# Two attention layers on one core: the second layer's output projection as Strassen products at the end, and log-sum rows by transfers

## The chip, the cores and the metric

The kernel runs on one core of one Trainium2 chip. The core has a matrix engine (TensorE, PE in the profile, with its weight loads shown apart as PEld), a vector engine (VectorE, DVE), a scalar engine (ScalarE, ACT), GpSimd (POOL) and a queue engine (SyncE, SP). SP, ACT and POOL issue DMA transfers, which 16 DMA engines carry out. The metric is the device time of one execution in microseconds; less is better.

## The reference

Two independent attention layers, A and B, each with an input `x` of 2048 x 1024, a `wqkv` of 1024 x 3072 and a `wo` of 1024 x 1024, all float32, with 32 heads of 32 features.

```
qkv = (x @ wqkv).reshape(B, S, 3, H, Dh)            # q, k, v per head
A: each position sees 8 keys: itself and every second position before it
   logits = q . k * scale, softmax over the 8, weighted sum of v, then @ wo
B: each position sees itself and the 255 before it
   scores = q . k * scale, masked, softmax, weighted sum of v, then @ wo
result = concat([a, b], axis=-1)
```

Both projections `@ wo` are full 2048 x 1024 by 1024 x 1024 matrix products. For A, the host sorts positions into even and odd ones, so that "every second position" becomes a plain window of 8 neighbours.

## The kernel before

**Units and groups.** The work is cut into 8 units of 512 positions: units 0 to 3 are layer B (`dense`), units 4 to 7 layer A (window of 8). A unit has 8 groups (`NG`) of four heads; a group is numbered `hg` = 8u + s. For each unit the program makes q and k per group (`qk_items`, L518), v in three parts (`v_items`, L583), attention per group, and the output projection (`o_items`, L645).

**Precision by three terms.** Each float32 operand of a large product is held as a high part and a low part in TensorE's faster type. `parts` (L195 to L209) makes them: a cast by ScalarE (L201) or VectorE (L204), then subtractions on VectorE (L207, 512 columns at a time). Every product is then three matmuls (`TERMS`): high x high, high x low, low x high.

**The stream of operands.** `Stream` holds the list of all weights and inputs in the order of their use, each item 128 x 1024 floats (512 KB). `load_to` issues a load on POOL's queue (L159) into one of three buffers (`raws`, `NRAW` = 3); `split_to` splits it into `wpool` (three tiles) or `xpool` (nine half tiles); when the split is over, the buffer takes the next load.

**Attention of layer B.** Per group, a first pass (`first`, L857) makes 16 score blocks, VectorE adds the mask and takes row maxima (L862), ScalarE sums the exponentials (L867). `log_sum` turns maximum and sum into one number per row, as a high and a low part (L885 to L888). `rows` turns these to lie along the free axis by a matmul with the identity (L896), and `spread` writes them as rows 96 to 127 of the stacked q, one VectorE multiplication for each of four heads (L902). A second pass (`second`, L940) of 128 rows then gives transposed scores less their log-sum in one matmul, ScalarE's exponential (L947) gives probabilities, GpSimd or VectorE clears what is masked (L926, L929), and L987 multiplies by v. The stacked q and k (`qst`, `kst`, two of each) are filled by SP's transfers out of `nat` (L479), halo reads (L408) and writes (L469).

**Attention of layer A.** `window`: q and k are seated by SP's transfers (L438), 128 small matmuls score (L711), VectorE and ScalarE do the softmax (L719 to L749), ScalarE spreads it (L758, L761), and L774 multiplies by v.

**Output.** `finish` splits each group's outcome into high and low (L822 on ScalarE, L826 on VectorE) in one of ten tiles of `opool`. The projection of unit u-1 runs between the groups of unit u (`O_SLOTS`), 8 outputs of 24 matmuls each; the last unit's projection stands at the very end, where four of its outputs are started without their last step (`TAIL`). `copy_out` (L536, L539) takes a finished output out of PSUM, and ACT's queue stores it.

**What sets the order.** A planner in the program (`Clock`, and the loop from L1060) knows a duration for each kind of work and writes all engines' instructions in the order of its due times. It takes from four lists: the long products (`gemm`), first passes, second passes, and the row matmuls. On the chip each engine runs its instructions in that written order and waits by semaphores.

Of the kernel before, what the change touches and what calls it, by code (L numbers as in the profile page):

```python
# [7 lines left out]
F32 = mybir.dt.float32  # L8
# [19 lines left out]
ROWS_LATE, KEYS_LATE = 0, 1.2  # L28
# [6 lines left out]
TAIL, XAT = 4, 1  # L35
# [95 lines left out]
class Stream:  # L131
# [3 lines left out]
    def __init__(self, nc, ck, raws, wpool, xpool, items, more, light):  # L135
# [4 lines left out]
        self.loaded = self.split = 0  # L140
# [3 lines left out]
    def load_to(self, n):  # L144
        while not self.loaded:
# [7 lines left out]
            self.loaded = 2  # L153
        while self.loaded < min(n, len(self.items)):
            k = self.loaded - NRAW
# [7 lines left out]
    def split_to(self, n):  # L163
# [12 lines left out]
        while self.split < min(n, len(self.items)):  # L176
            i = self.split
            self.load_to(i + 1)
            raw, t0 = self.raw.pop(i)
            if self.items[i][0] != "w":  # L180
                self.tiles[i], self.ready[i] = [], []
                for h in range(2):
                    t = self.xpool.tile([P, 2, S], F32R, tag="x", name="x")
                    self.ready[i].append(self.parts(t, raw[:, h * S:(h + 1) * S], t0, i < SIDE))
                    self.tiles[i].append(t)
# [31 lines left out]
def kernel(ctx, tc, xs, wqk, wv, wo, outs, units):  # L217
# [3 lines left out]
    U = len(units)  # L221
    units, xs = [units[i] for i in ORDER], [xs[i] for i in ORDER]
# [5 lines left out]
    natp = ctx.enter_context(tc.tile_pool(name="natp", bufs=NN))  # L228
    pickp = ctx.enter_context(tc.tile_pool(name="pickp", bufs=1))
    opool = ctx.enter_context(tc.tile_pool(name="opool", bufs=NO))  # L230
# [13 lines left out]
    for u in range(U):  # L244
        for s in range(NG):
            if u and s in O_SLOTS:
                plan += [("o", u - 1, n) for n in O_SLOTS[s]]
# [6 lines left out]
    plan += [("o", U - 1, n) for n in range(NG)]  # L254
    items, where = [], {}

# [13 lines left out]
    for p in plan:  # L270
        ly = units[p[1]][0]
        if p[0] == "o":
            item(p, "w" if p[1] < U - 1 or p[2] < 3 else "xw", wo[ly, p[2]])
# [25 lines left out]

    qst = [stackp.tile([P, 4, S], F32R, tag=f"q{i}", name=f"qst{i}") for i in range(2)]  # L300
# [4 lines left out]
    def constants():  # L305
# [13 lines left out]
        pick = cst["pick"] = pickp.tile([32, 16], F32, name="pick")  # L319
        nc.gpsimd.memset(pick, 0.0)  # L320
        for row in (0, 16):
            nc.gpsimd.affine_select(pick, pick, pattern=[[-1, 16]], compare_op=ALU.not_equal, fill=1.0, base=-row,
                                    channel_multiplier=1)
# [14 lines left out]
        def ones():  # L338
            zero = cst["mask_d"][96:P, None, P:2 * P].to_broadcast([32, 24, P])
            for t in kst:  # L340
                nc.scalar.activation(t[96:P, :, :].rearrange("p j (a s) -> p (j a) s", s=P), zero, AF.Identity,
                                     bias=1.0, scale=1.0)
                ck.use("act", 2.7, ck.now)
# [12 lines left out]
    xt, xready, ot, rows = {}, {}, {}, {}  # L356
    done, waiting = {}, {}
    for k in ("stack", "v", "o", "ot", "out", "nat", "second", "clear", "scores"):
        done[k] = {}
# [36 lines left out]
    def qk_items(u, s):  # L396
# [100 lines left out]
        for t in range(2):  # L497
# [15 lines left out]
            def run(k, t=t, h=h):  # L513
# [6 lines left out]
                if k == ASK and st.items[min(where["qk", u, s, t] + 1, len(st.items) - 1)][0] != "x":  # L520
                    st.split_to(where["qk", u, s, t] + 2)
# [100 lines left out]
    def o_items(u, n):  # L622
        h = {}

        last = u == U - 1
        ring = rs if last and n == 3 else rg

        def ready(k):
            if (u * NG + k) not in done["ot"]:
                return None  # L630
            if k == 0:
# [3 lines left out]
                return latest(ring.when(), h["r"][0], done["ot"][u * NG])  # L635
            return max(done["ot"][u * NG + k], h["r"][k // 4])

        def run(k):
            if k == 0:
                h["ps"], h["b"] = ring.take()  # L640
# [6 lines left out]
            if k == ASK and (not last or n == 0 or n > 2):  # L647
                st.split_to(where["o", u, n] + (3 if last and n == 0 else 2))
            if k == 5 and last and n in (1, 2):
                st.split_to(where["o", u, n] + 3)  # L650

        def after(k):
            if k == NK - 1:
# [3 lines left out]
                o = pbuf[:, n % 4, :S] if last else stp.tile([P, S], F32, tag="ost", name="ost")  # L657
                e = copy_out(o, h["ps"], h["b"], ring)
# [9 lines left out]
        return [(lambda k=k: ready(k), lambda k=k: run(k), 3 * CG, lambda k=k: after(k)) for k in range(NK)]  # L668

# [461 lines left out]
```

## Time and profile before

| | |
|---|---|
| median of 3 runs | 1832.38 us (1831.74 to 1832.67) |
| profiled execution, first to last instruction | 1830.6 us |
| TensorE busy | 1807.8 us, 99% |
| VectorE busy | 1202.9 us, 66% |
| ScalarE busy | 889.4 us, 49% |
| GpSimd busy | 394.4 us, 22% |
| DMA | 257.43 MB, 141 GB/s on average |

The profiled execution's own time is given by the page as its span only, 1830.6 us from the first to the last instruction; the three timed runs are other executions, 1.8 us longer in the median. A row of the groups by line has the line, engine and operation, what is written from what with the shapes, the count, then the busy time and the mean of one, then the idle time of the engine before them and what ended it. A row of the waits has who waited for whom, us in total, times, and the longest. A row of the timeline has start, length, engine, line, operation and count, with the idle time before it in brackets. A row of a DMA issue has the tile, the queue, the count, the size of one and the median us from issue to landing. A matmul's duration is modelled and overlaps the next one.

### The profile page before, as it was taken

The numbers are of one execution on the slowest core, as the hardware profiler recorded it, in microseconds if no ns is written. First come the engines' busy times: TensorE is split into PE (matmuls) and PEld (weight loads), VectorE is DVE, ScalarE is ACT, GpSimd is POOL, SyncE is SP. The second block draws the span as 40 slices with busy tenths as digits, with TensorE's granted clock in tenths as the row PEclk, the third lists the DMA queues.
The fourth block names the chain that finished last, engine by engine and source line by source line (L and its number), as shares of the span: only waits on it lengthen the run. The fifth ranks groups of instructions, "written<-read, shape, count | busy, mean of one in ns | idle before, by whom it ended". The sixth has DMA issues, their size and how long they took to land.

```text
span 1830.6 us, 38331 instructions
## 1 busy us (share of the span) xinstructions
PE 1807.8 (99%) x14826; PEld 1477.5 (81%) x14826; DVE 1202.9 (66%) x2694; ACT 889.4 (49%) x2254; POOL 394.4 (22%) x926
## 2 busy tenths in 40 slices
PE   9999999999999999999999999999999999999998
PEld 7787777888778888788887788888888788888887
DVE  6677886768867669777777564655547445655463
ACT  5556466565655655656555343433425234423331
POOL 3322323233242324332233200110001000100000
PEclk9999999999999999999999999999999999999999
DMA  8455665545656456455554343444334443534432
GB/s 242 121 138 139 176 164 150 170 121 160 164 155 164 136 151 183 125 157 141 141 142 130 110 135 116 152 143 130 119 115 143 133 138 108 162 107 128 127 104 83
DMA packets 109141, 257.43 MB, mean 141 GB/s; under 512 B 14496, under 2 KB 29856, under 8 KB 108960
## 3 DMA queue, kind: packets, MB, share of 16 engines
q0 software_dynamic: 41760, 152.06, 28.1%
q1 hardware_dynamic: 56832, 83.00, 17.6%
q10 hardware_dynamic: 10368, 19.93, 3.0%
q8 instruction: 117, 1.92, 0.5%
q14 instruction: 64, 0.52, 0.1%
HBM read 164.63 MB, written 23.07 MB: 103 GB/s over the span
## 4 chain that ended last, share of the span: by engine, by line
PE 92%; DVE 4%; DMA 2%; ACT 2%; issue 1%; SPq 0%; ACTq 0%; POOL 0%; DVEq 0%; POOLq 0%
PE g L518 37%; PE g L645 19%; PE g L583 17%; PE s L940 5%; PE s L857 5%; PE o L987 5%; PE s L711 2%; PE o L774 2%; DMA raw<-xs 1%; DVE w L207 1%; DVE s L862 1%; ACT s L867 0%; DMA qst<-nat 0%; DMA pbuf<-nat 0%; DVE x L207 0%
## 5 line engine op out<-in xcount | busy, mean ns | idle before, releaser
L518 PE MATMUL g<-x,w 128*128 128x512 f32 x3072 | 770.2, 394 | 3.8 <-DVE nm L729 2.4
L518 PEld LDWEIGHTS g<-x,w 128*128 128x128 f32 x3072 | 566.3, 189 | 114.2 <-issue 8.3
L583 PE MATMUL g<-w,x 128*128 128x256 f32 (+1 forms) x2304 | 391.9, 320 | 0.9 <-issue 0.7
L207 DVE TENSOR_TENSOR w<-raw,w 128x512 fp32r<-128x512 f32 x516 | 338.6, 698 | 52.0 <-ACT w L201 44.8
L583 PEld LDWEIGHTS g<-w,x 128*128 128x128 f32 x2304 | 332.3, 190 | 29.2 <-DVE w L207 1.8
L645 PE MATMUL g<-ot,w 128*128 128x512 f32 x1416 | 343.6, 393 | 3.7 <-DVE ot L826 1.8
L867 ACT ACTIVATE s<-s,nm 128x384 f32<-128x384 f32 (+2 forms) x512 | 274.3, 536 | 102.1 <-DVE nm L862 101.8
L862 DVE CUSTOM_DVE_ANT_0 s<-s,mask_d 128x384 f32<-128x384 f32 (+2 forms) x512 | 261.5, 553 | 88.2 <-PE s L857 87.5
L645 PEld LDWEIGHTS g<-ot,w 128*128 128x128 f32 x1416 | 262.4, 188 | 59.3 <-DVE ot L826 3.2
L926 POOL TENSOR_SCALAR_AFFINE_SELECT pbuf<-pbuf 128x128 f32<-128x128 f32 (+1 forms) x606 | 219.8, 391 | 325.1 <-ACT pbuf L947 323.8
L947 ACT ACTIVATE pbuf<-s 128x384 f32<-128x384 f32 (+2 forms) x480 | 202.7, 505 | 72.2 <-PE s L940 70.2
L159 POOL DMA_DIRECT2D raw<-wqk x126 | 68.1, 540 | 457.5 <-DVE w L207 356.3
L204 DVE CAST w<-raw 128x1024 fp32r<-128x1024 f32 x205 | 141.7, 691 | 24.8 <-PE g L518 24.0
L940 PEld LDWEIGHTS s<-qst,kst 128*128 128x128 f32 x704 | 113.0, 188 | 41.2 <-ACT s L867 16.3
L857 PE MATMUL s<-kst,qst 96*128 96x384 f32 (+2 forms) x512 | 142.4, 342 | 0.9 <-ACT s L867 0.6
L940 PE MATMUL s<-qst,kst 128*128 128x256 f32 (+2 forms) x704 | 136.5, 302 | 3.5 <-ACT s L867 3.0
L719 DVE TENSOR_TENSOR band<-s,near 128x160 f32<-128x160 f32 x128 | 32.4, 315 | 158.0 <-PE s L711 158.0
L536 ACT COPY ost<-g 128x512 f32<-128x512 f32 x54 | 31.7, 587 | 207.1 <-PE g L645 200.4
L857 PEld LDWEIGHTS s<-kst,qst 96*128 96x128 f32 x512 | 93.4, 189 | 26.2 <-issue 4.7
L826 DVE TENSOR_TENSOR ot<-o,ot 128x512 fp32r<-128x512 f32 x64 | 44.0, 688 | 101.6 <-ACT ot L822 101.4
L867 ACT ACTIVATION_READ_ACCUMULATOR s<-s,nm 128x1 f32 x512 | 105.3, 206 | 0.0
L159 POOL DMA_DIRECT2D raw<-wo x64 | 34.2, 534 | 304.2 <-DVE w L207 260.2
(77 smaller groups left out, 1298.6 us busy)
## 6 DMA issues: line engine op xcount, KB each, us to landing
raw<-wqk POOLq DMA_DIRECT2D x126, 512.0 KB, 4.3
raw<-wv POOLq DMA_DIRECT2D x72, 512.0 KB, 5.1
raw<-wo POOLq DMA_DIRECT2D x64, 512.0 KB, 4.1
qst<-nat SPq DMA_DIRECT2D x96, 256.0 KB, 5.3
kst<-nat SPq DMA_DIRECT2D x96, 256.0 KB, 5.6
raw<-xs POOLq DMA_DIRECT2D x28, 512.0 KB, 4.6
outs<-ost ACTq DMA_DIRECT2D x56, 256.0 KB, 2.3
kst<-halo SPq DMA_DIRECT2D x72, 128.0 KB, 4.5
```

Source lines behind the costliest of these rows:

```text
L159: (self.nc.scalar if early else self.nc.gpsimd).dma_start(raw if len(ap.shape) == 2 else raw.rearrange("p (a b) -> p a b", a=2), ap)
L204: nc.vector.tensor_copy(t[:, 0, :], raw)
L207: nc.vector.tensor_tensor(t[:, 1, c:c + 512], raw[:, c:c + 512], t[:, 0, c:c + 512].bitcast(F32), op=ALU.subtract)
L518: nc.tensor.matmul(h["ps"], h["w"][:, a, k * P:(k + 1) * P], xt[u][k][:, b, :], start=(k == 0 and i == 0), stop=(k == NK - 1 and i == 2))
L583: nc.tensor.matmul(ps, xt[u][kw * g + k][:, a, p0:p0 + P], h["w"][g][:, c, k], start=(first and t == 0 and half == 0), stop=(last and t == 2),
L645: nc.tensor.matmul(h["ps"], w[:, a, c:c + P], ot[u, k][:, b, :], start=(k == 0 and i == 0), stop=(k == NK - 1 and i == 2))
L857: nc.tensor.matmul(ps[:, :n], q[0:96, j, b * P:(b + 1) * P], kk[0:96, j, c0:c1], start=True, stop=True)
L862: nc.vector.tensor_tensor_reduce(ps[:, :n], ps[:, :n], mask[:, cut:full], scale=-1.0, scalar=BIG, op0=ALU.add, op1=ALU.min, accum_out=nm)
L867: nc.scalar.activation(ps[:, :n], ps[:, :n], AF.Exp, bias=nm, scale=-1.0, accum_out=sm)
L926: nc.gpsimd.affine_select(w, w, pattern=[[0, m], [step, n]], compare_op=ALU.is_ge, fill=0.0, base=base, channel_multiplier=chan)
L940: nc.tensor.matmul(ps[:, i * n:(i + 1) * n], kk[:, j, 256 + kb * P:256 + (kb + 1) * P], q[:, j, q0:q0 + n], start=True, stop=True)
L947: nc.scalar.activation(w, ps[:, :pack * n].rearrange("p (j n) -> p j n", j=pack), AF.Exp)
```

## The change

Two things change.

**Layer A's projection.** Units 4 and 5, and units 6 and 7, form pairs. In a pair, the outputs of attention are a matrix of 2 x 2 blocks (unit by half of the 1024 features), and so is `wo` (half of the features by half of the outputs). Of the eight block products only seven are made, out of blocks and sums of blocks, by a Strassen scheme (`PRODUCTS`), and added up into four blocks (`product`). Each product is 4 x 4 x 3 = 48 matmuls. All 14 stand at the end of the program. Outputs of layer A's attention are therefore not split at once: `finish` copies them out and SP stores them to DRAM (`od`). Sums of them (`output_sums`) and of `wo` (`weight_sums`) are made in the background by tasks of two loads, four VectorE operations and two stores (`background`), into `sd` and `td`, after unit 3's projection and whenever two units' outputs are stored. The products' operands come through the stream: two items of outputs or sums and two of weights or sums for each product; `gates` hold back a load in the written order until what it reads is stored. Finished blocks leave by ACT's queue out of three tiles in turn, or out of the tile in which they were added up. Unit 3's projection is spread over units 4 and 5 (`O_LATE`).

**Log-sum rows.** `spread` no longer multiplies. It copies the 32 x 128 outcome of the row matmul to one small tile, by ScalarE or VectorE, and SP copies it by four transfers into 8 rows (96 to 103) of the stacked q, one for each head. The rows of the stacked k that meet them hold ones only for the head's own two rows, and the second pass reads 104 rows instead of 128. The planner adds 2.0 us to the landing of each row transfer (`ROWS_LATE`).

Ten tiles of a new pool (`slot`) take the place of `opool` and serve outputs, sums, totals and outgoing tiles.

```diff
-ROWS_LATE, KEYS_LATE = 0, 1.2
+ROWS_LATE, KEYS_LATE = 2.0, 1.2
-TAIL, XAT = 4, 1
+PRODUCTS = (("11", "11"), ("12", "21"), (0, 3), (2, 2), ("22", 1), (3, 0), (1, "22"))
+O_LATE = {4: {2: (0, 1), 3: (2, 3)}, 5: {2: (4, 5), 3: (6, 7)}}
+BG_REST, BG_SLACK = 2.0, 1.5
...
-    plan += [("o", U - 1, n) for n in range(NG)]
+    plan += [("p", u, i) for u in range(DU, U, 2) for i in range(7) if u > DU or i not in O_AT.values()]
...
+    def product(u, i):
...
+        def run(n, k):
+            if k == 0:
+                h["ps"], h["b"] = rg.take()
+            w, x = held["t", u, i, n // 2][0], held["s", u, i, k // 2][0][k % 2]
+            c = S * (n % 2) + P * k
+            for t, (a, b) in enumerate(TERMS):
+                nc.tensor.matmul(h["ps"], w[:, a, c:c + P], x[:, b, :], start=(k == 0 and t == 0),
+                                 stop=(k == 3 and t == 2))
+            if k == 1:
+                at = where["p", u, i, "t", 1]
+                more_w = [kind for kind, _ in st.items[at + 1:at + 1 + (n + 1 if n else 0)]]
+                while more_w.count("w") > 1 + n // 2:
+                    more_w.pop()
+                st.split_to(at + 1 + len(more_w))
...
+            if i in (1, 4):
+                where_o["ot"] += 1
+                o = slot(2 + where_o["ot"] % 2)[:, :S] if where_o["ot"] % 3 else stp.tile([P, S], F32, tag="ost", name="ost")
+            if i == 0:
+                nc.scalar.copy(a, ps)
+                e = ck.use("act", 0.485, ck.now + ck.SEM)
+            elif i == 1:
+                e = add(o, a)
+                store(0, 0, o, e)
+            elif i == 2:
+                e = add(a, a)
+            elif i == 3:
+                e = add(c, a)
+            elif i == 4:
+                e = add(o, c)
+                store(1, 0, o, e)
+            elif i == 5:
+                e = add(c, c)
+                store(1, 1, c, e)
+                e = add(a, a)
+            else:
+                e = add(a, a)
+                store(0, 1, a, e)
+            rg.give(bank, e)
...
+    def background():
...
+        loads, ops, dst, key, who = bg["tasks"].pop(0)
+        t = [slot(4 + 2 * lane + z).rearrange("p (a s) -> p a s", a=2) for z in range(2)]
+        for c, ap in loads:
+            nc.sync.dma_start(t[c // 2], ap)
+            e = ck.copy("load", ck.now)
+
+        def add():
+            for to, x, y, op in ops:
+                nc.vector.tensor_tensor(*[t[c // 2][:, c % 2, :] for c in (to, x, y)], op=op)
+                e = ck.use("dve", 0.64, ck.now, port=True)
+            ck.defer(e, put)
+
+        def put():
+            for z in range(2):
+                nc.sync.dma_start(dst[:, 2 * z:2 * z + 2, :], t[z])
...
     def finish(u, s, h):
-        o = opool.tile([P, 2, S], F32R, tag="ot", name="ot")
+        if u >= DU:
+            o = slot(2 + hg % 2)[:, :S]
+            nc.scalar.copy(o, h["o"])
...
+                nc.sync.dma_start(od[u][:, s, :], o)
...
+                    if s >= 4 and u % 2:
+                        output_sums(u - 1, s - 4)
...
+            return
+        o = slot(hg).rearrange("p (a s) -> p a s", a=2).bitcast(F32R)
...
             def spread():
-                for j in range(4):
-                    nc.vector.tensor_tensor(q[96:P, j, :].rearrange("p (b s) -> p b s", s=P),
-                                            ps[0:32, None, 0:P].to_broadcast([32, 4, P]),
-                                            cst["pick"][0:32, 4 * j:4 * j + 4, None].to_broadcast([32, 4, P]), op=ALU.mult)
+                row = rowp.tile([32, P], F32R, tag="row", name="row")
+                if ck.ends("act", 0.22, ck.now) <= ck.ends("dve", 0.2, ck.now):
+                    nc.scalar.copy(row, ps[0:32, 0:P])
...
+                else:
+                    nc.vector.tensor_copy(row, ps[0:32, 0:P])
...
+                def place():
+                    h["rows"] = []
+                    for j in range(4):
+                        nc.sync.dma_start(q[96:104, j, :].rearrange("r (b s) -> r b s", s=P).bitcast(F32),
+                                          row.bitcast(F32))
+                        h["rows"].append(ck.copy("part", e, ck.now) + ROWS_LATE)
...
-                nc.tensor.matmul(ps[:, i * n:(i + 1) * n], kk[:, j, 256 + kb * P:256 + (kb + 1) * P],
-                                 q[:, j, q0:q0 + n], start=True, stop=True)
+                nc.tensor.matmul(ps[:, i * n:(i + 1) * n], kk[0:104, j, 256 + kb * P:256 + (kb + 1) * P],
+                                 q[0:104, j, q0:q0 + n], start=True, stop=True)
```

More of the change, by code (lines that the diff above doesn't have):

```diff
@@ L178, in split_to @@
             self.load_to(i + 1)
+            if i not in self.raw:
+                return
             raw, t0 = self.raw.pop(i)
@@ L221 @@
     U = len(units)
+    DU = sum(u[2] for u in units)
     units, xs = [units[i] for i in ORDER], [xs[i] for i in ORDER]
@@ L354 @@
     halo = [[dram.tile([P, 2, 256], F32, name=f"halo{i}_{s}") for s in range(NG)] for i in range(2)]
[L356 to L359, printed above, removed]
+    xt, xready, ot, rows, waiting = {}, {}, {}, {}, {}
     class Ring:
```

208 lines of the change are left out of this document (168 added, 40 removed).

## The prediction

> **What bounds the kernel now.** I read the page first: the busy shares, the granted clock, the chain that ended last.
>
> ```profile
> span 1830.6 us, 38331 instructions
> PE 1807.8 (99%) x14826; PEld 1477.5 (81%) x14826; DVE 1202.9 (66%) x2694; ACT 889.4 (49%) x2254; POOL 394.4 (22%) x926
> PEclk9999999999999999999999999999999999999999
> PE 92%; DVE 4%; DMA 2%; ACT 2%; issue 1%; SPq 0%; ACTq 0%; POOL 0%; DVEq 0%; POOLq 0%
> ```
>
> TensorE is busy for 99% of the span at full clock and carries 92% of the chain; the other engines have room on average. So a matmul taken away shortens the time, if nothing new makes TensorE wait. The span is 1.8 us under the median of the three runs (1832.38); I sum on the span and add 1.8.
>
> Next the timeline of TensorE at the end, for what one matmul costs when they follow each other closely and what the end loses; then its waits by releaser.
>
> ```profile
> 1786.00 7.54 PE L645 MATMUL g<-ot,w 128*128 128x512 f32 x32 [1.12 <-DVE ot L826]
> 1804.96 21.92 PE L645 MATMUL g<-ot,x 128*128 128x512 f32 x96
> ```
> ```profile
> PE s L896 <- DVE hl L888: 3.6, 4, 2.0
> PE s L940 <- ACT s L867: 3.0, 4, 1.1
> PE g L518 <- DVE nm L729: 2.4, 1, 2.4
> ```
>
> 96 matmuls of 512 columns in 21.92 us are 0.228 us each, though the rows give each 394 ns: they overlap. The waits are few. Two lie at the end: 2.4 us (the one wait on L729, in the last unit's attention) and 1.12 us before the projection. The 3.6 and 3.0 us lie in layer B, around the log-sum rows and the second pass.
>
> **The change, part by part.**
>
> *Matmuls.* Layer A's projection was 4 units x 8 x 8 x 3 = 768 matmuls of 512 columns; seven products for each of two pairs are 14 x 4 x 4 x 3 = 672. The built order shows exactly 96 fewer, every other matmul is still there, so a change that does not do what it says is ruled out here. 96 x 0.228 = **-21.9 us**, on the path, because TensorE is the path.
>
> *The end.* The last unit's attention no longer feeds the projection at once: pair 4's seven products (7 x 48 x 0.228 = 76.6 us) stand after the last units' matmuls and need only units 4 and 5. So the 2.4 and 1.12 us should mostly go: **-3 us**, between -1 and -4. What is late next is the last two sums of pair 6, wanted 76 us later. The very end, evacuation and one store, stays: an addition out of PSUM instead of a copy (688 against 587 ns below), 0.1 us.
>
> *Log-sum rows: work.* Per dense group four multiplications (676 ns) leave VectorE and one copy of 32x128, smaller than one of them, comes (22 on VectorE, 10 on ScalarE).
>
> ```profile
> L902 DVE TENSOR_TENSOR qst<-s,pick 32x512 fp32r<-32x512 f32 x128 | 79.3, 676 | 9.9 <-PE s L896 9.4
> 200.00:250.00 50.00, 48.42 (x257) 37.87 (x258) 40.94 (x111) 30.59 (x95) 14.54 (x38) 1.00 0.70 186
> 700.00:750.00 50.00, 48.78 (x306) 37.90 (x305) 42.50 (x114) 30.36 (x88) 15.51 (x31) 1.00 0.68 190
> ```
>
> (The first row is of the groups by line; the other two are 50 us windows: length, busy us of PE, PEld, DVE, ACT and POOL with their instructions, granted clock, DMA share, GB/s.) 128 x 0.676 = 86.5 us of VectorE go, where it is busiest: 41 to 42.5 us of 50 at the unit boundaries, where TensorE loses 1.6 and 1.2 us. But of the two waits named, one ends on ScalarE's exponentials (L867), and the other's L888 stands behind a logarithm of their sums. So I take **-2 us** of the 6.6 (between 0 and -6.6). K=104 instead of 128 in the second pass changes no column count: 0.
>
> *Log-sum rows: the new wait.* Four transfers of 16 KB on SP replace the multiplications. The nearest rows are SP's small stores into the seats and three issues in a row.
>
> ```profile
> pbuf<-nat SPq DMA_DIRECT2D x128, 65.0 KB, 4.4
> pbuf<-nat SPq DMA_DIRECT2D x128, 64.0 KB, 2.3
> 173.26 1.85 SPq L479 DMA_DIRECT2D qst<-nat  x3
> ```
>
> An issue takes 1.85/3 = 0.62 us. The first second-pass matmuls want the second transfer: copy up to 0.6, two issues 1.2, landing 2.3 to 4.4: 4.1 to 6.2 us after the rows' matmul. In the changed order 5.3 to 13.8 us of other matmuls stand there (counted at 0.228 us per 512 columns; 1.5 to 5.5 before). At 6.2 us four groups are short, by 0.9, 0.6, 0.4 and 0.2: 2.1 us in all. **+1 us**, between 0 and 2.1. Behind these transfers on SP wait the next group's stack copies, ten issues per group at most; with four more SP issues 14 x 0.62 = 8.7 us per group of about 30 us.
>
> *Units 4 to 7.* Unit 3's projection is spread over units 4 and 5, layer A's leaves. Each of 32 groups loses a VectorE subtraction (688 ns) and gains a 256 KB store on SP. Twelve sums (four of weights, eight of outputs) each load 1 MB, do four additions and store 1 MB: 48 x about 0.69 = 33 us of VectorE, nearly all in units 5 to 7, where it was half idle:
>
> ```profile
> 1650.00:1700.00 50.00, 50.00 (x499) 40.87 (x498) 28.41 (x47) 18.83 (x37) 4.75 (x9) 1.00 0.44 136
> ```
>
> SP now takes a sum's stores behind its additions, and the seats' transfers (scores wait for them) behind those. The seats go out some 10 us of matmuls ahead: **+1 us**, between 0 and 3.
>
> *The products.* The last 672 matmuls are 153.2 us. Each product loads and splits four items of 512 KB (two of sums or outputs, two of weights) in 10.9 us, 2.74 us per item, where one projection item had 5.5 us. The prices:
>
> ```profile
> L207 DVE TENSOR_TENSOR w<-raw,w 128x512 fp32r<-128x512 f32 x516 | 338.6, 698 | 52.0 <-ACT w L201 44.8
> L201 ACT CAST w<-raw 128x1024 fp32r<-128x1024 f32 x52 | 54.1, 1047 | 10.9 <-PE g L583 6.4 <-ACT ost L536 2.7 <-DVE band L731 0.7
> L201 ACT CAST x<-raw 128x512 fp32r<-128x512 f32 x31 | 17.8, 618 | 22.7 <-DMA raw<-xs 19.9 <-DVE x L204 2.6
> L826 DVE TENSOR_TENSOR ot<-o,ot 128x512 fp32r<-128x512 f32 x64 | 44.0, 688 | 101.6 <-ACT ot L822 101.4
> L536 ACT COPY ost<-g 128x512 f32<-128x512 f32 x54 | 31.7, 587 | 207.1 <-PE g L645 200.4 <-PE s L940 5.5 <-DMA kst<-nat 1.2
> ```
>
> VectorE: 112 low parts x 0.698 + 56 additions x 0.688 + 8 of the last two sums = 122 us of 153. ScalarE: 56 x 0.618 + 28 x 1.047 + 8 x 0.587 = 69 us. Neither is the bound; in the sixth product, with eight additions, VectorE needs 11.1 us of 10.9, which three PSUM banks carry. The loads decide:
>
> ```profile
> raw<-wo POOLq DMA_DIRECT2D x64, 512.0 KB, 4.1
> q0 software_dynamic: 41760, 152.06, 28.1%
> 0.00:50.00 50.00, 46.84 (x187) 35.93 (x188) 32.91 (x85) 27.78 (x66) 13.95 (x35) 0.97 0.79 232
> 1169.66 0.53 POOL L159 DMA_DIRECT2D raw<-xs  x1 [11.53 <-ACT x L201]
> 1193.08 0.70 POOL L159 DMA_DIRECT2D raw<-wv  x1 [0.97 <-DVE w L207]
> ```
>
> Three raw buffers give each 3 x 2.74 = 8.2 us for landing (4.1 to 4.5) and splitting (1.05 + 2 x 0.70 = 2.4, more when VectorE adds first): 6.5 to 7.6 us. That fits with little over. On the other side, the densest eight loads of this trace run from 1169.66 to 1193.08, 2.93 us each; at that pace 56 take 164 us, 11 more. By bytes: 56 x 0.524 + 32 stores x 0.262 + the last two sums' 4.2 and two stored outputs' 0.5 = 42.4 MB in 153 us, 277 GB/s; the load queue's own rate is 152.06 MB in 28.1% of the span, 296 GB/s. So **+5 us**, between 0 and 11, nearer the buffers' sum because the dense eight loads shared VectorE with attention.
>
> The Trainium skill, "DMA: Bandwidth & Descriptors", section "Anatomy of one DMA — SWDGE (gpsimd) path", gives 2.0 us plus bytes/436e3 for such a load, an estimate of 3.2 us for 512 KB. This trace's 4.1 us from issue to landing is longer and decides; by the page each buffer would have 1 us more and the sum would be 1807.5.
>
> Sum: 1830.6 - 21.9 - 3 - 2 + 1 + 1 + 5 = 1810.7; + 1.8 = **1812.5 us**. All terms at their low ends give 1800, at their high ends 1825.6.
>
> **The rivals.**
>
> *The products are paced by transfers.* For it: 277 GB/s asked for, and the first 50 us of this trace, full of loads, reached 232. Against: 296 on the load queue. At 250 GB/s the 42.4 MB take 170 us, 16.5 instead of 5 more: **1824**.
>
> *Slower: the rows arrive late in every group.* Place: first matmul of the second pass, 32 times; cause: the rows' four transfers stand on SP behind six stack copies of the next group (3.7 us by 0.62 each), so all four and a 4.4 us landing come 9 us or more after the rows' matmul. Over the counted distances a delay of 6.2 us costs 2.1, 7.4 costs 11.7, 8.0 costs 21, 9.0 costs 39. It decides from 8.0 us on, where it eats the gain; at 9.0: **1850**. For it: SP takes its issues in order. Against: in the changed order those copies are mostly released several us before the rows' matmul.
>
> *Slower: the clock falls.* If every product began with a wait longer than any in this trace, the clock could drop as it had at the start:
>
> ```profile
> 5.00:15.00 10.00, 8.55 (x22) 5.29 (x22) 7.90 (x12) 6.59 (x11) 6.17 (x13) 0.83 0.98 346
> L1055 PE MATMUL s<-qst 128*128 128x512 f32 x10 | 4.6, 645 | 1.5 <-DVE qst L1052 1.5
> ```
>
> A matmul there costs 4.6/10 = 0.46 us, 0.23 more than at full clock; some 13 of them (3.0 us) after each of 14 waits of over 2.4 us are 14 x 5.4 = 76 us: **1883**. The longest wait here, 2.4 us, left the clock at 1.00. The Trainium skill, "TensorE: Matmul & The Clock Gate", section "HAM oscillation — how this bites in real kernels", warns against idle gaps over about 3.4 us; the trace agrees as far as it goes (2.4 us did nothing).
>
> *More gain.* All 6.6 us of layer B's named waits go and the products never wait: **1803**.
>
> **How the numbers follow.** Forecast 0.58, paced products 0.17, late rows 0.15, clock 0.03, more gain 0.07. Time 1812.5 (own range 1805 to 1820). Range 1800 to 1831: outside lie the late rows and the clock, 0.18, and next to nothing below. No change means within 0.2%, 3.7 us, about what a measurement here can tell: only the far end of the paced products and the first of the late rows fall there, 0.03. Faster 0.80, same 0.03, slower 0.17.
>
> **What would show it.** Right: TensorE's matmuls at the end about 0.23 us apart over some 155 to 160 us, with short waits on VectorE's low parts; no wait on L711 or L729's work near the end; VectorE under 40 of 50 us in layer B; second-pass matmuls that do not wait for SP's row transfers. Wrong: loads landing after 6 us or more in the last 150 us with a DMA share over 0.9 (paced); a wait of several us at the second pass in most groups (late rows); a granted clock under 1 at the end. Waits in units 5 to 7 released by seats' transfers would show that the sums on SP cost what I put at 1 us.

## The result and the profile after

The changed kernel takes 1854.82 us in the median of 4 runs (1852.03 to 1855.95) where the kernel before, on the same chip, takes 1832.06 us (4 runs, 1831.66 to 1832.67). The ratio is 1.0123, 95% interval 1.0108 to 1.0137: 22.8 us slower, where 1812.5 us was forecast.

The page of the changed kernel, the span, the busy times and the engines' shares of the chain that ended last:

```profile
span 1850.3 us, 38789 instructions
...
PE 1806.6 (98%) x14730; PEld 1466.1 (79%) x14730; DVE 1185.6 (64%) x2666; ACT 924.8 (50%) x2313; POOL 401.4 (22%) x972
...
PE 16%; DMA 3%; issue 2%; DVE 2%; ACT 1%; POOL 0%; POOLq 0%; ACTq 0%; DVEq 0%
```

The 96 matmuls are gone (14826 to 14730), yet TensorE is busy for as long as before. The chain before was 92% TensorE's; the chain that the page follows now covers 24% of the span, 8% of it on other engines, issues and transfers. Where the time is spent shows in windows. The first row is the kernel before; the other three are the changed kernel, over the same stretch and in two of the 50 us windows that the prediction showed:

```profile
0.00:1050.00 1050.00, 1037.43 (x6463) 835.73 (x6464) 773.16 (x1972) 599.48 (x1713) 319.51 (x790) 1.00 0.55 152
```
```profile
0.00:1050.00 1050.00, 1027.98 (x6108) 823.29 (x6109) 685.62 (x1831) 594.62 (x1718) 305.26 (x804) 0.99 0.55 150
...
200.00:250.00 50.00, 47.27 (x258) 36.13 (x257) 31.75 (x86) 25.28 (x78) 11.89 (x31) 0.97 0.60 160
...
700.00:750.00 50.00, 47.41 (x295) 39.93 (x294) 40.24 (x101) 23.16 (x67) 15.70 (x31) 0.97 0.61 175
```

In 1050 us TensorE stands idle for 22.0 us instead of 12.6, and the clock's column is below 1.00. VectorE has become lighter as intended (773 to 686 us; the kernel before does about 19 us of layer A in this stretch, the changed kernel none). Layer B's last matmul with v starts at 1054.1 us; it was 1031.0. So layer B lost 23.1 us, and layer A, with 96 matmuls less, took 796.2 us instead of 799.6.

The six largest of TensorE's waits between 50 and 1080 us of the changed kernel, nearly all of it layer B, by what released them (us in total, times, longest):

```profile
PE s L1119 <- DVE hl L1111: 4.2, 4, 1.9
PE s L1080 <- DMA kst<-nat: 3.7, 2, 2.5
PE s L1080 <- ACT s L1090: 3.7, 6, 1.1
PE s L1174 <- ACT s L1090: 2.0, 1, 2.0
PE g L707 <- ACT r L1045: 1.9, 3, 0.8
PE s L1174 <- ACT pbuf L1181: 1.9, 3, 0.7
```

L1080 is the first pass (it was L857), L1119 the rows' matmul (L896), L1174 the second pass (L940), L1090 the exponential sums (L867), L707 the projection. In the whole list no wait is released by the row transfers. What is late are the stacked keys, the first pass's score banks, and the log-sums, a little each.

The timeline around the longest of them, and around the two longest of the products (L766), with start, length, count and the idle time before in brackets:

```profile
213.79 1.52 PE L647 MATMUL g<-w,x 128*128 128x512 f32 x6
217.82 0.63 PE L1080 MATMUL s<-kst,qst 96*128 96x128 f32 x4 [2.51 <-DMA kst<-nat]
218.29 2.73 PE L647 MATMUL g<-w,x 128*128 128x512 f32 x6
```
```profile
1692.69 5.59 PE L766 MATMUL g<-x,w 128*128 128x512 f32 x16 [3.17 <-ACT w L213]
...
1721.13 9.21 PE L766 MATMUL g<-x,w 128*128 128x512 f32 x27 [2.87 <-ACT w L213]
```

Six matmuls took 1.52 us ahead of the wait and 2.73 us behind it: the clock had dropped to half. The trace grants half the clock for 3.4 us each at 218.4, 474.4, 737.3 and 1693.0 us and for 6.8 us at 1720.3. The kernel before has none of these; both have one at the start (10 us) and one at the very end.

The end of the changed kernel, four windows of the products, and how the loads of the second one landed:

```profile
1680.00:1700.00 20.00, 16.75 (x64) 12.45 (x64) 12.40 (x19) 10.76 (x19) 3.09 (x5) 0.91 0.67 226
1700.00:1720.00 20.00, 18.12 (x113) 14.03 (x111) 12.66 (x20) 7.43 (x12) 3.17 (x6) 1.00 0.93 323
1720.00:1740.00 20.00, 18.87 (x71) 15.33 (x72) 15.66 (x25) 7.62 (x11) 3.17 (x6) 0.83 0.73 229
1740.00:1850.00 110.00, 105.28 (x459) 85.32 (x457) 71.39 (x115) 39.03 (x54) 19.19 (x33) 1.00 0.73 227
```
```profile
raw<-td POOLq DMA_DIRECT2D x3, 512.0 KB, 7.9
raw<-sd POOLq DMA_DIRECT2D x2, 512.0 KB, 7.0
```

From 1700 to 1720 us the last sums' loads and stores, finished outputs and the products' own loads ask for 323 GB/s at a share of 0.93; the loads of sums (`sd`, `td`) land after 7.0 and 7.9 us in the median, and TensorE's 2.87 us of idleness at 1721 follow. The 672 matmuls of the products went from 1677.6 to 1846.3 us, 0.251 us each; 0.228 was forecast, plus 5 us in all.

### The profile page after: what moved, and what is told of

Same layout as the page of the kernel before. It is cut to its first block, busy times and chain, and to the rows that moved or that the text cites. A ratio compares the mean times of both kernels' runs of the same rounds, so it can differ in the third digit from the quotient of the medians.

```text
span 1850.3 us, 38789 instructions
## 1 busy us (share of the span) xinstructions
PE 1806.6 (98%) x14730; PEld 1466.1 (79%) x14730; DVE 1185.6 (64%) x2666; ACT 924.8 (50%) x2313; POOL 401.4 (22%) x972
## 3 DMA queue, kind: packets, MB, share of 16 engines
q1 hardware_dynamic: 78592, 118.66, 23.2%
## 5 line engine op out<-in xcount | busy, mean ns | idle before, releaser
L579 PE MATMUL g<-x,w 128*128 128x512 f32 x3072 | 771.6, 395 | 6.4 <-ACT x L213 1.7
L579 PEld LDWEIGHTS g<-x,w 128*128 128x128 f32 x3072 | 566.3, 189 | 121.5 <-issue 9.8
L647 PEld LDWEIGHTS g<-w,x 128*128 128x128 f32 x2304 | 336.4, 191 | 29.7 <-DVE w L219 1.1
L1090 ACT ACTIVATE s<-s,nm 128x384 f32<-128x384 f32 (+2 forms) x512 | 274.1, 536 | 138.9 <-DVE nm L1085 137.4
L1160 POOL TENSOR_SCALAR_AFFINE_SELECT pbuf<-pbuf 128x128 f32<-128x128 f32 (+1 forms) x628 | 210.2, 364 | 270.3 <-ACT pbuf L1181 268.8
L707 PE MATMUL g<-r,w 128*128 128x512 f32 x768 | 196.1, 398 | 2.8 <-ACT r L1045 1.9
L707 PEld LDWEIGHTS g<-r,w 128*128 128x128 f32 x768 | 141.0, 188 | 34.2 <-ACT r L1045 2.7
L766 PE MATMUL g<-x,w 128*128 128x512 f32 x672 | 160.4, 399 | 7.6 <-ACT w L213 6.5
L766 PEld LDWEIGHTS g<-x,w 128*128 128x128 f32 x672 | 128.1, 192 | 39.4 <-ACT w L213 8.3
L1080 PE MATMUL s<-kst,qst 96*128 96x384 f32 (+2 forms) x512 | 141.0, 345 | 8.1 <-DMA kst<-nat 3.7
L1174 PEld LDWEIGHTS s<-qst,kst 104*128 104x128 f32 x704 | 112.8, 189 | 41.6 <-ACT s L1090 14.6
L216 DVE CAST w<-raw 128x1024 fp32r<-128x1024 f32 x186 | 128.4, 691 | 25.3 <-PE g L579 21.3
L1174 PE MATMUL s<-qst,kst 104*128 104x256 f32 (+2 forms) x704 | 136.7, 303 | 4.1 <-ACT s L1090 2.0
L1080 PEld LDWEIGHTS s<-kst,qst 96*128 96x128 f32 x512 | 93.0, 189 | 35.4 <-ACT s L1090 9.4
L213 ACT CAST w<-raw 128x1024 fp32r<-128x1024 f32 (+1 forms) x74 | 76.4, 1036 | 61.9 <-DMA raw<-wo 28.3
L1090 ACT ACTIVATION_READ_ACCUMULATOR s<-s,nm 128x1 f32 x512 | 105.1, 205 | 0.0
L924 DVE TENSOR_TENSOR band<-s,near 128x160 f32<-128x160 f32 x128 | 32.5, 317 | 110.5 <-PE s L916 110.5
```

The lines of the kernel that those rows point to most:

```text
L216: nc.vector.tensor_copy(t[:, 0, :], raw)
L579: nc.tensor.matmul(h["ps"], h["w"][:, a, k * P:(k + 1) * P], xt[u][k][:, b, :], start=(k == 0 and i == 0), stop=(k == NK - 1 and i == 2))
L647: nc.tensor.matmul(ps, xt[u][kw * g + k][:, a, p0:p0 + P], h["w"][g][:, c, k], start=(first and t == 0 and half == 0), stop=(last and t == 2),
L707: nc.tensor.matmul(h["ps"], w[:, a, c:c + P], ot[u, k][:, b, :], start=(k == 0 and i == 0), stop=(k == NK - 1 and i == 2))
L766: nc.tensor.matmul(h["ps"], w[:, a, c:c + P], x[:, b, :], start=(k == 0 and t == 0), stop=(k == 3 and t == 2))
L1080: nc.tensor.matmul(ps[:, :n], q[0:96, j, b * P:(b + 1) * P], kk[0:96, j, c0:c1], start=True, stop=True)
```

## The experiments

"Clock" is the mean granted clock over the runs of a kernel; span times (1 - clock) is what the dropped clock took, at most: the drop at 1720.3 us, for one, began while TensorE stood idle. "Distance" is from the start of the rows' matmul to the first matmul of the second pass in the trace, as a mean over groups 8 to 29. All were timed beside the kernel before, which had 1831.6 to 1832.6 us and clocks of 0.9975 to 0.998, some 4 us.

| run | edit | us | ratio (95%) | clock | distance |
|---|---|---|---|---|---|
| after | the change | 1854.8 | 1.0123 (1.0108 to 1.0137) | 0.992 | 9.2 |
| e1 | new rows alone | 1854.2 | 1.0122 (1.0099 to 1.0144) | 0.995 | 9.1 |
| e2 | products alone | 1835.5 | 1.0019 (1.0009 to 1.0029) | 0.994 | 3.6 |
| e3 | change, tiles moved 64 bytes | 1857.3 | 1.0134 (1.0118 to 1.0151) | 0.991 | 9.3 |
| e4 | change, no margin | 1849.8 | 1.0084 (1.0061 to 1.0107) | 0.993 | 7.5 |
| e5 | delay of 5.0 alone | 1871.5 | 1.0209 (1.0181 to 1.0237) | 0.990 | 9.5 |
| e6 | unread transfers | 1871.7 | 1.0221 (1.0205 to 1.0236) | 0.994 | 4.8 |
| e7 | products, six buffers | 1824.7 | 0.9960 (0.9946 to 0.9974) | 0.996 | 3.6 |
| e8 | e7, tiles moved | 1820.2 | 0.9939 (0.9924 to 0.9954) | 0.997 | 3.6 |
| e9 | short multiplications | 1834.7 | 1.0013 (1.0001 to 1.0025) | 0.997 | 3.6 |
| e10 | the same, delay of 5.0 | 1876.8 | 1.0245 (1.0229 to 1.0261) | 0.989 | 9.6 |
| e11 | unread transfers, copy on VectorE | 1841.9 | 1.0056 (1.0039 to 1.0074) | 0.997 | 3.7 |
| e12 | e8, additions later | 1833.5 | 1.0007 (0.9997 to 1.0017) | 0.994 | 3.6 |
| e13 | delay of 3.0 alone | 1853.6 | 1.0115 (1.0099 to 1.0132) | 0.995 | 6.3 |
| e14 | delay of 5.5 alone | 1857.0 | 1.0138 (1.0123 to 1.0153) | 0.994 | 9.2 |
| e15 | mask preference 0.25 | 1832.7 | 1.0002 (0.9992 to 1.0011) | 0.997 | 3.6 |
| e16 | keys' number 1.4 | 1827.4 | 0.9978 (0.9967 to 0.9990) | 0.998 | 3.6 |
| e17 | e1, mask preference 0.25 | 1856.7 | 1.0138 (1.0118 to 1.0157) | 0.995 | 9.2 |
| e18 | e8, keys' number 1.4 | 1823.1 | 0.9953 (0.9937 to 0.9969) | 0.995 | 3.6 |

**Which half of the change loses.** e1 puts the new rows (copy, four transfers, 104 rows, 2.0 us of margin) into the kernel before; e2 is the changed kernel with the four multiplications and no margin:

```diff
 e2, against the changed kernel
-ROWS_LATE, KEYS_LATE = 2.0, 1.2
+ROWS_LATE, KEYS_LATE = 0, 1.2
-                row = rowp.tile([32, P], F32R, tag="row", name="row")
...
-                        nc.sync.dma_start(q[96:104, j, :].rearrange("r (b s) -> r b s", s=P).bitcast(F32),
+                    nc.vector.tensor_tensor(q[96:P, j, :].rearrange("p (b s) -> p b s", s=P),
```

> The kernel before with the new log-sum rows alone (copy, four transfers, 104 rows, the planner's 2.0 us margin), layer A's projection as it was. Theory R (the rows' detour costs layer B its time: the second pass stands 5 to 14 us behind the row matmul instead of 1.5 to 5.5, everything that waits for it comes later): slower by 14 to 20 us, 1846 to 1852, nearly all before the last group of layer B, with about 18 us of the 23 us by which the changed kernel is behind at the end of layer B. Rival S (the loss in layer B comes from other things of the change, such as the new tiles of the projection): within 4 us of before.

> The changed kernel with the old log-sum rows (four VectorE multiplications, 128 rows, no margin). Theory R: layer B back to within 5 us of before, what is left being slower projection matmuls (about 6 ns each, 768 of them); layer A as in the changed kernel, about 3.5 us shorter than before: 1829 to 1837. Rival S: still about 23 us behind at the end of layer B, 1850 or more.

The rows alone took 1854.2 us, as much as both together and 2 us over theory R's range, and layer B ended at 1054.2 us as in the changed kernel. The products alone came to 1835.5, with layer B at 1032.7: the products gained nothing either, for reasons of their own (below).

**Two settings of the changed kernel.** The change allocates the pool of the attention outputs' tiles ahead of a 64-byte tile (`pick`) that stood ahead of it before. The projection's matmuls, whose moving operand these tiles are, start 233 ns apart in the changed kernel (median) and 227 in the kernel before. e3 allocates `pick` first again, which moves the tiles by 64 bytes; e4 drops the margin.

```diff
 e3
+    pickp = ctx.enter_context(tc.tile_pool(name="pickp", bufs=1))
     roomp = ctx.enter_context(tc.tile_pool(name="roomp", bufs=1))
-    pickp = ctx.enter_context(tc.tile_pool(name="pickp", bufs=1))
 e4
-ROWS_LATE, KEYS_LATE = 2.0, 1.2
+ROWS_LATE, KEYS_LATE = 0, 1.2
```

> The changed kernel with two pools in the other order, so that the ten tiles lie 64 bytes further, as the ten output tiles of the kernel before did; same instructions in the same order. Theory: the projection's matmuls in units 1 to 5 go from 233 ns back to 227, 768 x 6 ns = 4.6 us off: 1849 to 1852. Rival (the 6 ns come from what else runs beside them): no change, 1854 or more, and 233 ns stays.

> The changed kernel with the planner's margin on the row transfers at 0 instead of 2.0 us: the second pass is written 3 to 12 us of matmuls behind the row matmul instead of 5 to 14. Theory R: the margin is part of the detour, so some of the 18 us come back, 1842 to 1851, unless the transfers then land too late and TensorE waits for them at the second pass. Rival (the margin hides waits that would cost as much): 1855 or more, with waits at the first matmul of the second pass released by the row transfers.

In e3 the matmuls were 227 ns apart again, but the time did not fall (1857.3). Up to the end of layer B TensorE stood idle for 26.8 us there, 22.0 in the changed kernel, so the gain was lost again to other waits; why these grew is not shown. In e4 5 us came back. Its waits in layer B show what the margin had bought; here TensorE does wait for the row transfers:

```profile
PE s L1174 <- DMA qst<-row: 10.3, 9, 1.7
PE s L1080 <- DMA kst<-nat: 4.0, 2, 3.2
PE s L1119 <- DVE hl L1111: 2.5, 2, 1.3
```

**Is it the longer way or the transfers?** e5 has no new rows: only the planner is told that they come 5.0 us later. e6 keeps the old rows and adds the copy and four transfers that nobody reads.

```diff
 e5
-ROWS_LATE, KEYS_LATE = 0, 1.2
+ROWS_LATE, KEYS_LATE = 5.0, 1.2
 e6, behind the four multiplications
+                    nc.scalar.copy(row, ps[0:32, 0:P])
...
+                for j in range(4):
+                    nc.sync.dma_start(unused[hg][j], row.bitcast(F32))
```

> The kernel before with one number changed: the planner is told that the four multiplications' rows are there 5.0 us later (ROWS_LATE 5.0 for 0), so it writes the second pass further behind the rows' matmul: 8.8 us on average in the written order of the steady groups, where the changed kernel has 8.7 and the kernel before 3.5. Work, transfers, VectorE's load and K=128 stay. Theory D (the longer way from rows to second pass is what costs layer B: with two stack buffers a group cannot start until the second pass two groups back is done, and what is put into the longer way is missing elsewhere): most of the rows change's loss comes back, layer B ends at 1046 to 1056 us, the time is 1846 to 1856. Theory Q (the transfers, SP's queue and the copy are what costs): layer B ends at 1029 to 1035, the time is 1829 to 1837.

> The kernel before, with the row copy and the four SP transfers of the changed kernel added in every dense group, but into memory that nobody reads; the second pass still takes its rows from the four multiplications, at the distance of before. Theory D (the longer way costs): 1830 to 1838 us, layer B ends at 1031 to 1036. Theory Q (copy, SP's queue and the transfers cost): layer B ends at 1043 or later and the time is 1844 to 1856. In between both have a part.

The delay alone cost 40 us, more than theory D's range. Two of its waits in layer B:

```profile
PE s L857 <- ACT s L867: 10.7, 11, 1.8
PE s L896 <- DVE hl L888: 7.6, 3, 2.8
```

They are of the kind that the changed kernel has. e6 fell outside both theories and tested something else: the planner put every copy on ScalarE behind VectorE's multiplications, and ScalarE's queue stood there with the next exponentials behind it, as its waits show:

```profile
ACT row L911 <- DVE qst L904: 83.0, 23, 5.4
...
PE s L859 <- ACT row L911: 15.6, 11, 2.8
```

e11 repeats it with the copy always on VectorE. In both the transfers end in DRAM and not in the stacked q.

> The unread transfers once more (order and multiplications of the kernel before), with the 32x128 copy always on VectorE behind the four multiplications, so that it cannot hold ScalarE's queue as it did (83 us of waiting in front of 23 copies). VectorE gets 32 x 0.28 = 9 us more. If the copy in front of the exponentials was the whole loss there: 1831 to 1838 us, layer B ends at 1031 to 1037. If the four transfers and SP's queue cost by themselves: 1843 or more.

It took 1841.9 us, 9.6 more than before, between the theories. So the copy and the transfers are not free, even unread, but they do not carry the loss by themselves: without a longer way (3.7 us) 9.6 us of some 22 are there.

**What is VectorE's relief worth?** Each multiplication writes 32 of its 512 columns, in the written order of the kernel before (e9) and of e5 (e10).

```diff
-                    nc.vector.tensor_tensor(q[96:P, j, :].rearrange("p (b s) -> p b s", s=P),
+                    nc.vector.tensor_tensor(q[96:P, j, :].rearrange("p (b s) -> p b s", s=P)[:, :, 0:8],
```

> The kernel before in its own written order, but each of the four log-sum multiplications writes 32 of its 512 columns (the rest of the log-sum rows stays zero, so this kernel's output is not the attention's): what layer B gains when VectorE loses most of that work and nothing else changes. As the prediction had it (-2 us, at most -6.6): 1825.5 to 1832. If VectorE's queue is worth more than its waits show: 1812 to 1825. Layer B ends at 1031 less the same difference.

> The same shortened multiplications (the same rows left zero) in the order that the 5.0 us delay gives, which took 1871.5 us with the full multiplications. It is the changed kernel's rows without its copy and transfers. Theory D+R (the loss of the rows change is the longer way, less what VectorE's lighter queue gives back in that tighter order; the transfers cost next to nothing): 1846 to 1858 us, as the rows alone (1854.2), and layer B ends at 1046 to 1058. If the delay's loss does not hang on VectorE: 1863 to 1873, and then the transfers must be what made the rows alone faster, which nothing speaks for. If the transfers and SP's queue carry the loss: under 1843.

No gain in either (1.0013; 1876.8 against 1871.5 on another chip, above every range of e10's expectation). That VectorE's load explains the difference between the delay's 40 us and the rows' 22 is refuted.

**Does the loss follow the distance, or does any other order lose?** e13 and e14 are e5 with 3.0 and 5.5. e15 and e16 change numbers that do not concern the rows; e17 is e1 with the change of e15.

```diff
 e15 (and e17)
-MASK_BIAS = 0.2
+MASK_BIAS = 0.25
 e16
-ROWS_LATE, KEYS_LATE = 0, 1.2
+ROWS_LATE, KEYS_LATE = 0, 1.4
```

> The kernel before with the planner's delay of the log-sum rows at 3.0 us: the second pass is written 5.9 us on average behind the rows' matmul in the steady groups (3.5 before, 8.8 at 5.0). If the loss follows the distance from the start, in proportion: (5.9 - 3.5) / (8.8 - 3.5) = 0.45 of 40 us, 1850. If there is a slack that the first 2 to 3 us use up for nothing (the two stack buffers turn in 14.9 us on average and cannot in under 12.5): 1830 to 1840. If it hangs on the order and not on the distance: anything from 1830 to 1870, without relation to the other delays.

> The same with a delay of 5.5 us: the planner writes another order with the same average distance (8.77 us, where 5.0 gave 8.82 and the changed kernel has 8.71). If the distance carries the loss of 40 us: 1864 to 1878. If the order that the planner happens to write carries what is over the changed kernel's 22 us: away from 1871 by 8 us or more, between 1845 and 1863 or above 1880.

> The kernel before with the planner's preference between GpSimd and VectorE for the masks at 0.25 instead of 0.2: another written order, the same work, and the second pass still 3.5 us behind the rows' matmul on average. If the longer way costs (theory D): 1829 to 1837. If the order of the kernel before is a lucky one among its neighbours (theory T): 1842 to 1865.

> The kernel before with the planner told that the keys' stack copies land 0.2 us later (KEYS_LATE 1.4 for 1.2): another written order, mean distance 3.5 us. Theory D: 1829 to 1837. Theory T: 1842 to 1865.

> The new log-sum rows alone (1854.2 us) with the preference for the masks at 0.25: another order with nearly the same way. Theory D: 1848 to 1860. Theory T: it scatters, by 5 us or more from 1854 to either side.

Other orders with the short way run as the kernel before does or slightly better (1832.7, 1827.4); other orders with the long way lose 21 to 25 us (1853.6, 1857.0, 1856.7), and one 40 (e5; e10, in its order, 44.5). So the loss goes with the longer way, and the order of the kernel before was not a lucky one among the two neighbours tried. It is not proportional: at a distance of 6.3 us 21 us are lost, and at 9.2 hardly more. Its size also hangs on the written order: e4, at 7.5 us, is 14.3 us over e2, which has the same products and the short way, and the 15 us more of e5 did not come back in e14.

**The products.** e7 is e2 with six load buffers from the second product on, e8 also moves the tiles as e3 did.

```diff
+            j = self.loaded - self.deep
+            if j >= 0 and j % 2:
+                k = j // 2 % len(self.more)
             raw = self.more[k] if 0 <= k < len(self.more) else self.raws.tile([P, 1024], F32, tag="raw", name="raw")
```

> The seven products with the old log-sum rows (1835.5 us), and from the second product on every second load goes into a third of the window scores' buffer, which is free by then: six load buffers instead of three. Theory L (loads that land after 7 to 11 us instead of 4 find only three buffers, so TensorE waits, and the clock drops behind the longest wait): no wait over 1.5 us behind 1675 us, the 672 products' matmuls at 0.228 to 0.238 us on average instead of 0.253, the time 1822 to 1829. Theory B (bytes or the splits' engines pace the products): the mean stays at 0.245 or more, the time 1831 to 1837.

> The six-buffer kernel, and the tiles of the attention outputs moved by 64 bytes, back to the position in a 256-byte line that they had in the kernel before. The projection's matmuls of layer B at 227 instead of 233 ns: 768 x 6 ns = 4.6 us. If they lie on the path, the time is 3 to 5 us under the six-buffer kernel, 1817 to 1825 if that comes out as theory L has it; if not, it is the same within 1.5 us.

Both came out as theory L had it: 1824.7 and 1820.2 us, the second 11.8 us under the kernel before and 34.6 under the changed one. The products' matmuls took 0.2345 and 0.2327 us each, and this is all that TensorE waits for behind 1660 us in e8, with the window of the whole stretch:

```profile
PE o L981 <- ACT wide L970: 1.4, 1, 1.4
PE g L770 <- ACT w L218: 0.4, 1, 0.4
```
```profile
1660.00:1817.00 157.00, 151.53 (x699) 123.95 (x697) 112.16 (x180) 63.60 (x93) 27.10 (x48) 0.99 0.76 258
```

All queues together moved 258 GB/s on average in this stretch, and the products' matmuls waited once, for 0.4 us. e8 is 4.5 us faster than e7, about the 768 x 6 = 4.6 that the address is worth, where e3 had gained nothing; but up to 2.2 of the 4.5 are clock (7.7 against 5.5 us of span), so the two cannot be told apart here. Behind layer B the other waits lie in units 4 to 7: 2.6 us at most each, 13.5 in all. e12 put the sums' additions later in the written order to mend those around 1345 and 1366 us:

```diff
-BG_REST, BG_SLACK = 2.0, 1.5
+BG_REST, BG_SLACK = 2.0, 8.0
```

> The six-buffer kernel with the tiles moved (1820.2 us), and the four additions of a background sum put 8 us instead of 1.5 behind their loads in the written order. VectorE stood 6.5 us at 1343 us in front of such an addition whose 1 MB had not landed, with the next unit's x splits behind it, and TensorE then waited 3.8 us there, 2.5 us at 1366. If those waits come from the additions: 3 to 7 us less, 1813 to 1817, and no wait over 1.5 us between 1330 and 1370. If they come from the loads themselves, which land 7 to 8.5 us after their issue there: within 1.5 us of 1820.

A miss: 1833.5 us in the median of 12 runs, whose profiled one took 1827.2. There the waits at 1342, 1344 and 1364 us stayed (1.6, 1.5 and 1.7 us), so they do not come from the additions; between 1330 and 1368 us ScalarE stood 6.3 us for loads of x. And now TensorE waited for low parts and additions at 1660 and 1694 us (2.05 and 1.73). e18 changes layer B's order under e8.

> The six-buffer kernel with the tiles moved and the old log-sum rows (1820.2 us), in the order that the keys' 1.4 gives. If the gain of the products and that of the order add: 1820 less 2 to 6, 1814 to 1818. If they do not: 1819 to 1826; if the products' gain hung on the one order of layer B: 1828 or more.

1823.1 us: the products keep their gain in another order; e16's gain is not added.

## Why the prediction was wrong

**Matmuls, -21.9 us.** Right in number and price: 96 fewer, 227 ns apart. Even e8, though, shows only 11.8 us of it as time; units 4 to 7 (below) took most of the rest.

**The step that failed: "Log-sum rows: the new wait", +1 us.** It priced the wait at the second pass for the transfers, and the runs show that wait not to be there in the changed kernel (none released by the row transfers) and to be 10.3 us without the margin (e4). What it took as cover, "5.3 to 13.8 us of other matmuls" in between, was counted as free because the matmuls have to be made anyway. They do, but a longer way from rows to second pass holds the group's stacked q and k longer, and there are two of each. From a group's last second-pass matmul to the first first-pass matmul two groups on, which reuses its stack, the traces have 14.85 us on average and 13.0 at least before the change, 13.3 and 12.5 with it (groups 8 to 29; e13's expectation took 12.5 for a floor, but e14 has 11.2 once). Of the 5.5 us of longer way 4.4 were taken from there (1.5), from the length of the first pass (24.6 to 23.2), the second (14.7 to 13.7) and the way to the rows (0.6). The rest went into the cycle of a stack, which is two groups long: a group's period grew from 31.75 to 32.5 us, which would be 24 us over all 32 groups; layer B lost 23.1. Passes written closer together met their banks, exponentials and keys unfinished: the small waits at L1080 and L1119. Up to the end of layer B TensorE stood idle for 22.0 us instead of 11.7, and the three drops of the clock took up to 5.1; what made the rest of the 23.1 us stays open (3.5 at most can be the tiles' address, 576 x 6 ns, and e1, without it, lost as much). e5, e13 and e14 show that the longer way alone costs 21 us or more, e15 and e16 that other orders without it cost nothing. That the two stacks are what makes the cycle short is read from these times and not tested; no run has a third pair.

**The rivals.** "The rows arrive late in every group" had a similar price, 1850, by chance: its mechanism was rows that come 8 us or more behind their matmul. The last of the four transfers was issued 2.8 to 3.2 us behind it in 25 of the 32 groups and 6.8 us at most, and the second pass, 5.9 to 16.1 us behind it, found the rows there. "The clock falls" was given 0.03 and the price 1883; its mechanism came true in small. The changed kernel's runs have a mean clock of 0.992, 14.4 us of span, the kernel before, where it was timed beside e1, 0.998 and 3.7 us: up to 10.7 of the 22.8 us are clock. The 2.4 us that "left the clock at 1.00" did not prove that such waits are safe.

**VectorE's relief, -2 us.** Nothing (e9). VectorE did fall under 40 of 50 us in every window of layer B except one of 40.24, but its queue had not been what the waits were for.

**Units 4 to 7, +1 us, and the end, -3 us.** From layer B's end to the first product the forecast has 618.5 us: layer A's 799.6 - 21.9 - 3 + 1 + 5 = 780.7, less the products' 158.2 and 4.0 behind them. The changed kernel took 623.5, 5 us more, 192 x 6 ns = 1.2 of them by the tiles' address. e8 took 627.0, 8.5 more. TensorE's waits in this stretch, units 4 to 7, add up to 6.2 us in the kernel before, 10.3 in the changed kernel and 13.5 in e8; so "+1 us, between 0 and 3" was too small. The end's term held in the changed kernel: neither wait, 2.4 nor 1.12 us, is there.

**The products, +5 us.** The right mechanism, mis-sized: 0.251 x 672 = 168.7 us against 153.2 + 5. Four waits of 0.5 to 3.2 us, 7.3 in all, and the clock at two of them (3.4 + 6.8 us at half, 5.1) make 12.4 of the 15.5 us over 153.2. The sum took a landing of "4.1 to 4.5" for every load. When the last sums and the finished outputs share the queues it went up to 9.5, and three buffers do not carry that; six do, with 3.2 us over 153.2 in e8. The paced-products rival put it on the bytes, and its sign came true (loads landing after 6 us or more at a DMA share over 0.9). But e2 and e7 move the same bytes and differ by the buffers alone, and their products' matmuls take 0.253 and 0.2345 us: depth was short, not bandwidth.

The three errors add up: 24.1 us in layer B (1054.1 against 1031.0 - 2 + 1), 5.0 in units 4 to 7, 10.5 in the products are the 39.6 us between the forecast span of 1810.7 and the 1850.3 measured.

## What to carry to other kernels

Price a longer way in a pipeline by what it holds (here two stacks of q and k), not only by whether other work stands beside it: a step that arrives in time can still cost, because everything else in the buffers' cycle is written closer together. When work is moved to the end, look at what else transfers there and size the load buffers by the landing time under that load. A wait of TensorE costs itself and often the clock behind it: in these runs 49 of 102 waits of 1.5 us or more had a drop beside them.

## What the runs showed of the hardware

**The clock dropped behind waits much shorter than expected.** Over the profiled executions of both kernels and all experiments, TensorE's idle times behind the first 15 us were set against the drops to half clock that began during them or within 1.5 us of their end: of 254 between 0.6 and 1.5 us 6 had a drop, of 49 between 1.5 and 2.0 us 15, of 25 between 2.0 and 2.5 us 11, of 20 between 2.5 and 3.0 us 16, and of 8 longer ones 7. A drop lasted 3.4 us or a multiple of it; ten of the 64 drops had no such idle time over 0.6 us. The Trainium skill, "TensorE: Matmul & The Clock Gate", section "HAM oscillation — how this bites in real kernels", puts the limit at idle gaps of about 3.4 us; these runs do not agree, and the measurement decides. Runs of one kernel differed in the same way: e5 ran in 1862.6 us at a clock of 0.994 and in 1873.8 us at 0.987.

**A moving operand's address changed a matmul's pace.** With the tiles where the changed kernel, e2, e4 and e7 have them, projection matmuls of 512 columns started 233 ns apart; with the tiles moved by 64 bytes and nothing else changed (e3 against the changed kernel, e8 against e7), 227 ns, as in the kernel before. Only these two places were seen.

**A load of 512 KB landed after 3.7 to 11.3 us,** in e2's last 230 us, depending on what shared the queues. The estimate by the Trainium skill, "DMA: Bandwidth & Descriptors", section "Anatomy of one DMA — SWDGE (gpsimd) path", 3.2 us, was not reached in the products.
